# Nine products without a reader between the stages of the first chunk's first joins

## The chip, the cores and the metric

The kernel runs on one core of one Trainium2 chip. The metric is the device time of one execution in microseconds. Beside it stands the profile of one execution, whose span runs from the first recorded instruction to the last.

## The reference

```python
# attention: q, k, v of (4, 8, 768, 48), beta of (4, 8, 768)
k_n = k / (norm(k) + 1e-6)
for t in range(768):                       # one 48 x 48 state for each of 32 heads
    y[t]  = q[t] @ state
    v_old = state^T k_n[t]
    state = state + beta[t] * outer(k_n[t], v[t] - v_old)
# then two matrix products on x = y as (3072, 384)
h = x @ w_in                               # (384, 2048)
out = (h * sigmoid(h)) @ w_out             # (2048, 384)
```

Everything is float32.

## The kernel before

**Tiling.** The 768 tokens of a head are cut into six chunks of 128 tokens, and a chunk into two halves of 64. Inside a half the recurrence is a triangular system, which the kernel solves by inverting triangular blocks. The inverses of blocks of 16 by 16 are made by row updates on VectorE (`invert_first`, L726 to L765, for the first chunk), and are then joined on TensorE: first to blocks of 32, then to blocks of 64. The heads stand in two groups g of 16 heads (two batches each).

**The joins of the first chunk.** `joins(hf)` (L1818) does that for half `hf`, as ten stages in a fixed order:

| Stages | Function | TensorE products, tile | Who takes them out of PSUM |
|---|---|---|---|
| 1, 2 | `corner(0)`, `corner(1)`, L776 | 32 each, 32x32 by 16 columns, L782 | VectorE, two operations each, L789 |
| 3, 4 | `turned(0)`, `turned(1)`, L794 | 16 each, 32x32 by 32, L798 | one on ScalarE, one on VectorE (`by_act`, `by_dve`, L600, L603) |
| 5 | `straight(0)`, L806 | 32, 32x32 by 32, L811 | two on ScalarE, two on VectorE |
| 6 | `merge_half(0, first)`, L858 | 16, 32x32 by 32, L871, `py` | one on each |
| 7 | `straight(1)` | 32 | two on each |
| 8 | `merge_half(1, first)` | 16, `py` | one on each |
| 9, 10 | `merge_half(0, second)`, `merge_half(1, second)` | 16 each, `px` | one on each |

`turned(g)` reads what the evacuation of `corner(g)` wrote; `merge_half(g, first)` reads what that of `turned(g)` wrote; `merge_half(g, second)` reads what the evacuations of `straight(g)` and of `merge_half(g, first)` wrote. After stage 10 `inner` (L900, products `pz`, L905) reads the joined blocks, group 0 and then group 1, and `first_outputs` (L940, `py`, L951) and the transposes of the next chunk (`pt`, L556) follow.

**Float32 products.** A float32 product of TensorE stands in the trace as two MATMUL rows and two LDWEIGHTS rows: the eight products of `busy` in this kernel are x16 rows. Below, a row count is a count of these.

**Order.** The order of every engine's instructions is written out: `pin` (L80) chains each instruction behind the one pinned before it on the same engine. Between the stages of the joins stand other jobs, one entry of a list for each stage. `fetched` puts the loads of the second chunk's queries and of four pieces of `w_in` on the SP queue. `sized` scales a half of `v` on GpSimd (L511, which waits for the last VectorE instruction before it), copies keys there (L613), and begins the next weight piece. A weight piece is brought into shape (`narrow`, L257) by two ScalarE operations (L261, L262; this is what "begin" issues), two VectorE operations (L266, then L270) and one on GpSimd (L274); `fill` takes the oldest piece one step on: `filled(2)` issues L266 here, `filled(1)` issues L270, `begin_next` issues L261 and L262 of a later piece.

**PSUM.** `bank(room, name)` (L63) takes the next bank of a ring. The rings A and CC have three banks each; a join stage takes one of A (evacuated by ScalarE, except in `corner`) and one of CC (evacuated by VectorE). A bank is written again only when its last reader is done.

**`busy(n)`** (L377, matmul at L381) issues n products of the identity with the first state tile, 128x128 by 384 columns, into the next bank of CC. Nothing reads them. Before the change eight of them stand ahead of the joins: three at the start, and five one by one before `corner(0)`.

**Afterwards** the same joins run for the second half (`rest = joins(1)`), cut in pieces by a script (L1925) that puts runs of the first big matrix product (`hidden`, `phid`, L1114, 128x128 by 256, six rows in a run) between them.

Of the kernel before, what the change touches and what calls it, by code (L numbers as in the profile page):

```python
# [19 lines left out]
def kernel(  # L20
# [42 lines left out]
    def bank(room, name):  # L63

        tag = room[0]
        room.rotate(-1)
        return pools.get(tag, banks).tile([P, 512], FP32, name=name, tag=tag)
# [3 lines left out]
    def behind(later, earlier, how=NoSync):  # L71

        tc.add_manual_dep(
            later.ins, earlier.ins.name,
            mybir.DependencyInfo(how, mybir.DependencyReason.DATA), reason="order",
        )
# [3 lines left out]
    def pin(op):  # L80

        engine = op.ins.engine
        if engine in pins:
            behind(op, pins[engine])
        pins[engine] = op
        return op
# [23 lines left out]
    def together(*parts):  # L110
        for _ in zip_longest(*parts):
            pass
# [93 lines left out]
    def deep(fetch, *args, n=2):  # L206

        depth.append(n)
        fetch(*args)
        depth.pop()  # L210
# [166 lines left out]
    def busy(n=1, after=None, how=NoSync):  # L377

        for _ in range(n):
            pw = bank(CC, "pw")  # L380
            done = pin(nc.tensor.matmul(  # L381
                pw[:, 0:DM], lhsT=ident[:],
                rhs=states[0][:].rearrange("p u a d -> p (u a d)"), start=True, stop=True,
            ))
            if after is not None:
                behind(done, after, how)
                after = None
# [470 lines left out]
    def merge_half(g, hf, second):  # L858

        y = ys[0][:, g]  # L860
        pms = [bank(room, "px" if second else "py") for room in (A, CC)]
        for i in range(HH // 2):
            for e in range(2):
                n, k = 2 * i + e, hf ^ e ^ g
                even, odd = slice(W * k, W * k + T), slice(W * k + T, W * (k + 1))
                if second:
                    to, left, right = even, y[odd, n, :], xis[g][odd, n, T:W]
                else:
                    left = aps[0, g][0][even, n // H, n % H, T:W]
                    to, right = odd, xes[0][even, g * HH + n, :]  # L870
                yield pin(nc.tensor.matmul(  # L871
                    pms[k][to, T * i : T * (i + 1)], lhsT=left, rhs=right, start=True, stop=True
                ))
        for k, by in enumerate((by_act, by_dve)):
            e, half = hf ^ k ^ g, slice(W * k, W * k + T) if second else slice(W * k + T, W * (k + 1))
            of = pms[k][half, 0 : HH // 2 * T].rearrange("p (h t) -> p h t", t=T)
            by(xis[g][half, e::2, T:W] if second else y[half, e::2, :], of)
# [808 lines left out]
    def fill(n):  # L1686

        for _ in range(n):
            if not queue:
                return  # L1690
            piece = queue[0]
            piece.begin()
            piece.done += 1
            if piece.done > 1:
                next(piece.steps)
            if piece.done == 3:
                narrowed.append(piece.name)
                queue.popleft()
                for i in freed:
                    fetch_w_out(i)  # L1700
                freed[:] = {
                    ("in", 4): [0], ("in", 5): [1], ("in", 7): [4], ("out", 2): [5], ("out", 3): [6], ("out", 4): [7]
                }.get(piece.name, [])
                if eager and queue and queue[0].name in raws:
                    soon.append(queue[0])
            elif eager and piece.done == 1 and len(queue) > 1 and queue[1].name in raws:
                soon.append(queue[1])
# [110 lines left out]
    def joins(hf, between=()):  # L1818

        for stage in (  # L1820
            corner(0, hf), corner(1, hf), turned(0, hf), turned(1, hf), straight(0, hf), merge_half(0, hf, False),
            straight(1, hf), merge_half(1, hf, False), merge_half(0, hf, True), merge_half(1, hf, True),
        ):
            yield from stage
            for what in between[:1]:
                for one in what if isinstance(what, tuple) else (what,):
                    one()
            between = between[1:]
# [4 lines left out]
    def filled(n):  # L1833
        return lambda: fill(n)

    def fetched():
        deep(load_q, 1, n=3)
        for i in (3, 4, 5, 6):
            deep(fetch_w_in, i)
# [6 lines left out]
    def none():  # L1846
        pass

    together(joins(0, [none, fetched, none, sized, filled(2), none, filled(1), none, begin_next, none]))

    pieces = chained(hidden(0, 0), hidden(0, 1), project())

# [289 lines left out]
```

## Time and profile before

| What | Value |
|---|---|
| Time, median of 3 runs | 620.34 us (620.26 to 621.63) |
| The profiled execution | 622.65 us |
| Its span | 620.9 us |
| Mean granted TensorE clock of the profiled execution | 0.986 |
| TensorE rows MATMUL, LDWEIGHTS | 9538, 9538 |
| Span of the ten stages on TensorE, first start to last end | 26.83 to 41.04 us |

The profiled execution is 1.75 us longer than its span and 2.31 us longer than the median of the runs without a profile. In the rows below, PE is TensorE's matmul, PEld its weight load, DVE VectorE, ACT ScalarE, POOL GpSimd and SP the engine that issues most DMAs. A row of the timeline gives the start, the stretch that the merged instructions cover, engine, line, operation, tile names, shape and count; in brackets stands the idle time before it and what ended it, where "issue" means that the profile shows nothing that the engine waited for. PEclk is the granted TensorE clock as a share of full speed.

### The profile page before, as it was taken

The page shows a single profiled execution, that of the slowest core. Times are in us where ns is not written, and L with a number is a line of the kernel's source. Part 1 is how long each engine was busy: PE and PEld are TensorE (multiplying, and loading weights), DVE is VectorE, ACT ScalarE, POOL GpSimd, SP SyncE. Part 2 cuts the span into 40 slices and gives each one's busy share as a digit, 9 for nine tenths or more (in the row PEclk, how much of TensorE's full clock was granted, in tenths as well). Part 3 has the DMA queues.
Part 4 walks back from the last instruction along what each step waited for, and adds up shares of the span by engine and source line. Part 5 has one row for each costly group of instructions (what it writes and reads, how often), then busy time and mean ns, then how long its engine had stood idle before and what let it go on. Part 6 is the DMA issues. An engine that isn't in the chain of part 4 may idle for free.

```text
span 620.9 us, 21925 instructions
## 1 busy us (share of the span) xinstructions
PE 603.6 (97%) x9538; PEld 528.4 (85%) x9538; DVE 494.8 (80%) x1031; ACT 245.5 (40%) x559; POOL 82.8 (13%) x83
## 2 busy tenths in 40 slices
PE   8779999999999999999999999999999999999997
PEld 5677788766689988998899998898998899998997
DVE  5845888998979986768986859886859898797875
ACT  3654756143361133444332543333534323534500
POOL 5442621246100010000010000010000020000000
PEclk9958999999999999999999999999999999999999
DMA  7845665064426474236064436073533060110002
GB/s 157 183 93 157 207 137 138 29 176 113 108 50 126 87 151 72 61 61 149 0 123 105 111 78 128 1 143 74 124 82 71 1 111 21 35 28 1 1 1 52
DMA packets 144416, 55.07 MB, mean 89 GB/s; under 512 B 113584, under 2 KB 137776, under 8 KB 144320
## 3 DMA queue, kind: packets, MB, share of 16 engines
q1 hardware_dynamic: 143520, 52.80, 38.3%
q8 instruction: 75, 1.23, 0.9%
q10 hardware_dynamic: 800, 0.87, 0.5%
q14 instruction: 21, 0.17, 0.1%
HBM read 40.99 MB, written 10.49 MB: 83 GB/s over the span
## 4 chain that ended last, share of the span: by engine, by line
PE 96%; issue 2%; DVE 1%; ACT 0%; POOL 0%; DVEq 0%; POOLq 0%
PE phid L1114 14%; PE px L1455 14%; PE py L1455 10%; PE hu L1168 10%; PE hx L1168 8%; PE po L1375 7%; PE px L1614 4%; PE pa L585 4%; PE hu L1335 3%; PE hx L1335 3%; PE pz L905 3%; PE ph L893 2%; PE pyc L986 2%; PE pyc L973 2%; PE pu L925 2%
## 5 line engine op out<-in xcount | busy, mean ns | idle before, releaser
L1114 PE MATMUL phid<-xT,w_in 128*128 128x256 f32 x384 | 90.7, 389 | 0.1
L1114 PEld LDWEIGHTS phid<-xT,w_in 128*128 128x128 f32 x384 | 71.7, 192 | 10.9 <-issue 0.7
L688 DVE SCALAR_TENSOR_TENSOR rank<-g,step,x 128x31 f32<-128x31 f32 (+15 forms) x124 | 49.7, 400 | 4.2 <-DMA g<-blocks 1.2
L1455 PE MATMUL px<-sums_of_w,sums_of_g 128*128 128x192 f32 x256 | 46.5, 332 | 0.0
L693 DVE TENSOR_TENSOR x<-x,rank 128x31 f32<-128x31 f32 (+15 forms) x124 | 42.5, 342 | 4.4
L1455 PE MATMUL py<-w_out,sums_of_g 128*128 128x192 f32 x256 | 45.4, 329 | 0.0
L1455 PEld LDWEIGHTS px<-sums_of_w,sums_of_g 128*128 128x128 f32 x256 | 41.4, 190 | 1.2 <-issue 0.7
L1455 PEld LDWEIGHTS py<-w_out,sums_of_g 128*128 128x128 f32 x256 | 41.7, 190 | 0.6 <-issue 0.2
L521 POOL TENSOR_TENSOR vf<-vf,n_slot 128x768 f32<-128x768 f32 x10 | 15.4, 1552 | 190.6 <-DVE sums_of_g L1432 97.2
L1168 PE MATMUL hx<-xT,w_in 128*128 128x256 f32 x144 | 36.0, 379 | 0.0
L600 ACT COPY gT<-hu 128x512 f32<-128x512 f32 x36 | 21.1, 585 | 32.9 <-PE hu L1168 22.9
L1168 PE MATMUL hu<-xT,w_in 128*128 128x256 f32 x144 | 34.0, 379 | 0.0
L600 ACT COPY xT<-pyc 48x128 f32<-48x128 f32 (+2 forms) x120 | 31.1, 259 | 1.6
L932 DVE TENSOR_TENSOR state<-state,pu 48x384 f32<-48x384 f32 x44 | 24.3, 552 | 8.3 <-PE pu L925 7.3
L1168 PEld LDWEIGHTS hu<-xT,w_in 128*128 128x128 f32 x144 | 27.4, 190 | 3.7
L1168 PEld LDWEIGHTS hx<-xT,w_in 128*128 128x128 f32 x144 | 27.3, 190 | 3.6
L1122 ACT ACTIVATE gT<-phid 128x512 f32<-128x512 f32 x24 | 14.4, 600 | 36.6 <-PE phid L1114 34.3
L905 PEld LDWEIGHTS pz<-vf,xi 64*64 64x64 f32 x768 | 25.3, 142 | 3.5 <-issue 3.1
L1183 DVE TENSOR_TENSOR gT<-gT,hx 128x512 f32<-128x512 f32 x24 | 16.4, 685 | 13.3 <-PE hx L1168 13.1
L905 PE MATMUL pz<-vf,xi 64*64 64x48 f32 x768 | 27.0, 226 | 0.0
L1466 DVE TENSOR_TENSOR o<-o,kept 128x192 f32<-128x192 f32 (+1 forms) x24 | 10.1, 422 | 20.1 <-ACT kept L1463 20.0
L1432 DVE TENSOR_TENSOR sums_of_g<-gT 128x512 f32<-128x512 f32 (+2 forms) x36 | 22.6, 662 | 2.3 <-PE py L1455 2.2
(338 smaller groups left out, 1334.9 us busy)
## 6 DMA issues: line engine op xcount, KB each, us to landing
vf<-in_v_dram SPq DMA_DIRECT2D x48, 96.0 KB, 2.7
out_dram<-o SPq DMA_DIRECT2D x36, 96.0 KB, 2.3
w_out<-in_moe_w_in_dram SPq DMA_DIRECT2D x12, 256.0 KB, 3.4
sums_of_w<-in_moe_w_out_dram SPq DMA_DIRECT2D x8, 384.0 KB, 4.2
blocks<-ap SPq DMA_DIRECT2D x40, 64.0 KB, 2.4
g<-blocks SPq DMA_DIRECT2D x4, 512.0 KB
up<-x SPq DMA_DIRECT2D x4, 512.0 KB, 3.2
xi<-up SPq DMA_DIRECT2D x16, 128.0 KB, 3.5
```

Source lines behind the costliest of these rows:

```text
L585: pin(nc.tensor.matmul(pa[e][half, p * n * W : (p + 1) * n * W], lhsT=kq[rows, p, 0, half], rhs=kq[rows, p, js[0] : js[-1] + 1, half], sta ...
L600: return pin(nc.scalar.copy(to, of))
L688: pin(nc.vector.scalar_tensor_tensor(out=tv, in0=g[:, 0:m, m : m + 1].to_broadcast([P, m, n]), scalar=step[:, m : m + 1], in1=x[:, m : m + ...
L693: yield pin(nc.vector.tensor_tensor(out=x[:, 0:m, m:T], in0=x[:, 0:m, m:T], in1=tv, op=ALU.add))
L905: yield pin(nc.tensor.matmul(pz[rows, n * D : (n + 1) * D], lhsT=xis[g][rows, u * H + 2 * p + e, :], rhs=vfs[c][rows, hf, g * HB + u, p, : ...
L932: pin(nc.vector.tensor_tensor(out=to, in0=to, in1=by_heads(pu[of]), op=ALU.add))
L1114: pin(nc.tensor.matmul(ph[:, j * GT : (j + 1) * GT], lhsT=w_in[:, a, (2 * f + j) * P : (2 * f + j + 1) * P], rhs=xTs[c, hf][:, a, :], star ...
L1168: pin(nc.tensor.matmul(to[:, GT * i : GT * (i + 1)], lhsT=weights[:, f], rhs=moving, start=start and i == 0, stop=True, skip_group_check=True,
L1335: pin(nc.tensor.matmul(to[:, GT * i : GT * (i + 1)], lhsT=weights[:, 2 * u + i], rhs=moving, start=start and i == 0, stop=True, skip_group ...
L1375: pin(nc.tensor.matmul(pos[i][:, 0:DM], lhsT=hidden_of(0, hf, f // 2)[:, at : at + C], rhs=w_outs[f // HFF][:, f % HFF, :], start=(f == 0) ...
L1455: pin(nc.tensor.matmul(to, lhsT=at, rhs=quarter(f, *b) if isinstance(b, tuple) else sums_of_w[b][:, f], start=start and n == 0, stop=n == ...
L1614: pin(nc.tensor.matmul(acc, lhsT=hidden_at(g)[:, r], rhs=out_weights_at(w)[:, r], start=start and r == 0, stop=r == 3, skip_group_check=Tr ...
```

## The change

A tuple of two jobs takes the place of one in three entries of the list: after stage 2, `fetched` is followed by `busy(4)`; after stage 4, `sized` is followed by `busy(3)`; after stage 7, `filled(1)` is followed by `busy(2)`. The list is that of the first half; the joins of the second half are as before. No other instruction is added or taken away. Each of the nine products takes the next bank of the ring CC, so the banks of CC that the later stages get are others than before.

```diff
+    def steadied(n):
+        return lambda: busy(n)
+
...
-    together(joins(0, [none, fetched, none, sized, filled(2), none, filled(1), none, begin_next, none]))
+    together(joins(0, [none, (fetched, steadied(4)), none, (sized, steadied(3)), filled(2), none, (filled(1), steadied(2)), none, begin_next, none]))
```

`joins` ran a tuple's entries one after the other before the change already.

## The prediction

> **What bounds the kernel now.** I read the page first, for its engine table, its slices, its queues and its chain.
>
> ```profile
> PE 603.6 (97%) x9538; PEld 528.4 (85%) x9538; DVE 494.8 (80%) x1031; ACT 245.5 (40%) x559; POOL 82.8 (13%) x83
> ...
> PEclk9958999999999999999999999999999999999999
> ...
> q8 instruction: 75, 1.23, 0.9%
> ...
> PE 96%; issue 2%; DVE 1%; ACT 0%; POOL 0%; DVEq 0%; POOLq 0%
> ```
>
> TensorE bounds the kernel: 96% of the chain that ended last is PE, so time lost or won on PE early on is still there at the end. The granted clock is low only in slices 3 and 4 (15.5 us each); the joins of the first half lie there. Next comes the timeline of PE through those joins and `inner`.
>
> ```profile
> 27.79 1.03 PE L782 MATMUL pl<-sums_of_w,ap 32*32 32x16 f32 x94 [0.48 <-issue]
> 28.75 1.44 PE L798 MATMUL pl<-sums_of_w 32*32 32x32 f32 x33
> 32.12 0.95 PE L798 MATMUL pl<-sums_of_w 32*32 32x32 f32 x26 [1.93 <-issue]
> ...
> 36.40 1.00 PE L811 MATMUL pl<-sums_of_w 32*32 32x32 f32 x57 [1.58 <-issue]
> ...
> 39.90 1.14 PE L871 MATMUL px<-xi,xe_y 32*32 32x32 f32 x32 [0.98 <-DVE xe_y L603]
> 40.97 3.54 PE L905 MATMUL pz<-vf,xi 64*64 64x48 f32 x62
> ```
>
> PE stands still for 1.93, 1.58 and 0.98 us, the first two times for nothing that the profile names. The table of the stretches between these stops shows what they share.
>
> ```profile
> 27.79:30.20 2.41, 2.37 (x127) 2.20 (x127) 1.88 (x6) 0.81 (x2) 2.41 (x3) 1.00 0.57 118
> 32.12:34.82 2.70, 2.70 (x128) 2.56 (x128) 1.00 (x3) 1.54 (x3) 2.34 (x3) 0.50 0.55 103
> 36.40:38.92 2.52, 2.52 (x127) 2.39 (x126) 1.84 (x5) 1.16 (x4) 0.83 (x1) 0.50 0.63 127
> ```
>
> (Columns: stretch, length, busy time and count of PE, PEld, DVE, ACT, POOL, then PEclk, DMA share, GB/s.) Each holds 127 or 128 matmuls. On the page, the queue q8 carries instructions in 75 packets; 9538 + 9538 PE rows over 75 are 254, or 127 matmuls with their loads. I read the stops as PE without instructions: a block of 127 matmuls is used up in 2.4 to 2.7 us, but blocks begin 32.12 - 27.79 = 4.33 and 36.40 - 32.12 = 4.28 us apart. The third stop ends with VectorE's `xe_y`.
>
> The clock is the second thing. Single microseconds date its turns:
>
> ```profile
> 30.00:31.00 1.00, 0.19 (x5) 0.14 (x3) 0.42 (x1) 0.36 (x1) 1.00 (x2) 0.92 0.76 143
> 44.00:45.00 1.00, 1.00 (x51) 1.00 (x53) 0.34 (x2) 0.00 (x0) 0.00 (x0) 0.75 0.40 79
> 54.00:55.00 1.00, 0.78 (x28) 0.77 (x28) 0.38 (x1) 0.33 (x2) 0.00 (x0) 0.87 0.65 193
> 58.00:59.00 1.00, 1.00 (x8) 0.95 (x7) 0.00 (x0) 0.71 (x2) 0.00 (x0) 0.93 0.26 90
> ```
>
> With 0.50 as the low value, 0.92 puts the drop at 30.84 and 0.75 the rise at 44.50; 0.87 and 0.93 give a second dip from 54.74 to 58.14. The first lasts 13.66 us, the second 3.40, a quarter of it.
>
> **The change part by part.** *Added on PE:* nine products, 18 rows of 128x128 by 384. Their length comes from the big product's runs and from the rows of `pw` itself.
>
> ```profile
> 55.27 2.93 PE L1114 MATMUL phid<-xT,w_in 128*128 128x256 f32 x6
> ...
> 60.36 1.56 PE L1114 MATMUL phid<-xT,w_in 128*128 128x256 f32 x6
> ```
>
> ```profile
> L381 PE MATMUL pw<-state,ident x16: 486/590/1009, 2.1 to 26.4; 128*128 128x384 f32 x16
> ```
> The run of six in the second dip takes 2.93 - 1.56 = 1.37 us more than one at full clock: 0.23 us a row of 256 columns, and 0.34 for 384. The upper end is 0.49, the shortest `pw` row by itself. I take 0.34, since rows of a series overlap, and 0.1 for each series' start: 2.8, 2.1 and 1.5 us, together 6.4. At half clock a row costs 0.68, and 18 of them 12.2.
>
> *What lies beside them.* I carry the stages forward with the row spacings of before: `turned` 0.028 us ((0.95 - 0.24) / 26), `straight` 0.0135, the merges 0.017 at full clock (below: 1.13 for 56 rows) and 0.029 at half. Instruction blocks still begin at 32.12 and 36.40, but each boundary lies earlier among the stages, by 8, 14 and 18 rows.
>
> ```profile
> 68.00 1.13 PE L871 MATMUL px<-xi,xe_y 32*32 32x32 f32 x56
> ```
>
> - *Four products* take the place of `turned(0)` at 28.75 and end at 31.55. VectorE's evacuation of `corner` is done by then, so the third product's bank is free. 24 rows of `turned(0)` run to 32.2, and the next block is there at 32.12: the stop of 1.93 us is filled. `turned(1)` ends at 33.3 (33.0 before).
> - *Three products* run to 35.4. They need the banks that VectorE empties of `turned`, 0.42 us of work on an idle engine. `straight(0)` ends at 36.3, 2.4 us later than before. 18 of the 32 rows of the first merge are in the old block; they end at 36.6, after 36.40, so the stop of 1.58 us is gone too. `straight(1)` ends at 37.7, 0.5 us late.
> - *Two products* start at 37.8. Here VectorE is late next, and its queue is:
>
> ```profile
> 34.23 0.87 DVE L603 COPY xi<-pl 32x256 f32<-32x256 f32 x2 [0.62 <-PE pl L811]
> 35.12 1.34 DVE L266 TENSOR_SCALAR w_in<-w_in 128x768 uint32<-128x768 uint32 x1
> 36.50 0.43 DVE L603 COPY xe_y<-py 32x256 f32<-32x256 f32 x1
> 37.53 0.86 DVE L603 COPY xi<-pl 32x256 f32<-32x256 f32 x2 [0.60 <-PE pl L811]
> 38.43 0.96 DVE L270 SCALAR_TENSOR_TENSOR w_in<-sums_of_w_in,w_in 128x768 uint32<-128x768 uint32 x1
> 39.42 0.43 DVE L603 COPY xe_y<-py 32x256 f32<-32x256 f32 x1
> ```
>
> It begins at 36.55, 2.3 us later, and has no pause: 36.55 + 0.87 + 1.34 + 0.43 + 0.86 + 0.96 + 0.43 = 41.45, where before it ended at 39.85. This is 1.6 us later, because two pauses of 0.6 are used up. The second product waits for the bank of the first merge (39.2), the merge behind it for the bank that VectorE empties of `straight(1)` (40.05); both lie beside this queue. `merge_half(1, second)` starts at 41.5 in place of 39.90.
>
> *The clock.* Why it falls is read from three stretches of the length of the short dip, each ending at a turn:
>
> ```profile
> 27.43:30.84 3.41, 2.37 (x127) 2.20 (x127) 2.63 (x6) 1.49 (x3) 3.41 (x4) 1.00 0.56 112
> 51.32:54.74 3.42, 2.59 (x115) 2.26 (x115) 1.52 (x5) 0.65 (x2) 0.00 (x0) 1.00 0.45 132
> 41.08:44.49 3.41, 3.41 (x72) 3.41 (x75) 0.91 (x2) 0.83 (x2) 0.29 (x1) 0.50 0.65 120
> ```
>
> Ahead of both drops PE was busy for 70 to 76%, with 32x32 tiles nearly alone; ahead of the rise it was full, with 64x64. In the new order the stretches from 27.43, 30.84, 34.26 and 37.67 hold 2.1, 1.6, 1.1 and 1.3 us of full-array rows, so I take the clock as held. Then `merge_half(1, second)` takes 0.55 in place of 1.07 and ends at 42.05. The rows of `pz` take 0.027 in place of (3.54 - 0.30) / 61 = 0.053 us.
>
> *Behind the joins.* ScalarE brings the next wait:
>
> ```profile
> 39.22 0.88 ACT L261 ACTIVATE w_in<-w_out 128x768 f32<-128x768 f32 x1
> 40.01 0.97 ACT L262 ACTIVATE w_out<-w_out,plus 128x768 int32<-128x768 uint32 x1
> 41.08 0.36 ACT L600 COPY xi<-px 32x256 f32<-32x256 f32 x1
> ```
>
> L261 and L262 stand between its evacuations of the two second merges and last 1.76 us. Before, the stop of 0.98 us covered them. Now the first of these evacuations runs from 41.3 to 41.65, the pair to 43.35, the second to 43.75. Group 0 of `pz` runs from 42.05 to 42.9; group 1 waits until 43.8 and ends at 44.8 with its drain, against 44.51 before. **Sum: 0.3 us later.** With 0.49 a row the same walk ends 1.3 us later; with L266 at half its length (POOL idle) and no wait on ScalarE, 0.6 earlier.
>
> On GpSimd the scaling of `v` (L511) moves with the VectorE instruction ahead of it by under 1 us; `pz` needs it only after 42. The SP queue keeps its order, the products issue no DMA, and no load waits for them. Behind `pz`, PE is full (chain above), so 0.3 us stays. The sum is made on the profiled execution, 622.65 us with a span of 620.9 to become 621.2; the median of the runs is 2.31 us lower, and I add the 0.3 to that: **620.6 us.**
>
> [...] No row here shows the supply itself; the distance of 127 matmuls speaks for it.
>
> **The rivals.**
> 1. *Forecast:* stops filled, clock held through the joins, new waits on VectorE and ScalarE; second dip as before. +0.3 us; -0.6 to +1.3.
> 2. *The second dip goes as well.* The 3.42 us ahead of it hold small tiles nearly alone, between a `phid` run with transposes and the next run. With the stages 0.3 us later, full-array rows of its edge fall into that stretch. +0.3 - 1.37 = -1.1, 619.3 us. For it: the small tiles last barely as long as the 3.4 us between two turns. Against: the move is small.
> 3. *More than that:* the second dip goes and ScalarE and VectorE don't hold `pz` (-0.6 - 1.37 = -2.0), 618.4 us.
> 4. *The clock dips after the joins, slower:* at full clock `pz` fills only half of the stretch 41.08 to 44.49, where at half clock it filled all of it. If that is too little, the clock falls at 44.5 for one window, over the transposes:
>
> ```profile
> 44.50:47.91 3.41, 1.75 (x14) 1.51 (x15) 1.00 0.49 154
> ```
>
> (PE and PEld rows of L556 alone.) 14 rows of 128 columns are 1792, against 1536 that cost 1.37 us in the second dip: 1.6 us more. +1.9, 622.2 us. [...]
> 5. *The clock isn't held:* products at 0.68 a row from 30.84 on. `turned(1)` ends at 33.9, the three products at 38.0, `straight(1)` at 40.6, two products at 43.3, the merges at 45.8; then `pz` is 3.0 (full clock) to 4.7 us late. +3.9, 624.2 us. Against: 1.1 us or more of dense rows in each window.
> 6. *The change doesn't do what it says:* the stops aren't instruction supply and stay where the stages are. 1.6 + 1.93 + 1.58 = 5.1 later at the last merge, less 0.5 and 0.8 by the clock: +3.8, 624.1 us.
>
> **How the numbers follow.** Chances: 0.45, 0.20, 0.08, 0.12, 0.08, 0.07. A measurement of this kernel can tell about 0.3%, 1.9 us, from no change. Faster: case 3 and a seventh of case 2, 0.11. Slower: cases 5 and 6 and somewhat over half of case 4, 0.22. Within: 0.67. The range from 618.5 to 622.9 takes in cases 1, 2, 4 and most of 3, and leaves out 5 and 6.
>
> **What would show it.** Right: no stop marked issue between 31 and 37; PEclk 1.00 from 30 to 44; `pw` rows about 0.34 apart; `merge_half(1, second)` at about 41.5 behind DVE; group 1 of `pz` behind ACT at about 43.8. Wrong: PEclk 0.50 while products run (case 5) or right after 44.5 (case 4); stops of 1.5 us or more at the old stages (case 6); PEclk 1.00 from 54 to 58 (cases 2, 3). The sum is wrong, too, if instruction blocks arrive later than at 32.12 and 36.40.

## The result and the profile after

| Comparison | Changed | Before, same chip | Ratio (95% interval) |
|---|---|---|---|
| First | 627.58 us (median of 4, 626.06 to 628.46) | 620.41 us (4) | 1.0102 (1.0076 to 1.0128) |
| Again, `after_again` | 624.10 us (12, 622.28 to 628.27) | 620.69 us (30, 617.64 to 624.85) | 1.0054 (1.0026 to 1.0082) |

The change makes the kernel slower, by 0.5% where more runs were taken. Forecast was 620.6 us, no difference that can be told. The first ratio is the larger, but it rests on four executions of each kernel: in the second row single executions of the kernel before spread over 7 us, while the first four happened to lie within 1.4. The ratios are not quotients of the two medians, and differ from them by up to 0.2%.

The page of the changed kernel, in the lines that were read first before:

```profile
PE 608.8 (97%) x9556; PEld 530.2 (85%) x9556; DVE 494.3 (79%) x1031; ACT 245.9 (39%) x559; POOL 82.8 (13%) x83
...
PEclk9897999999999999999999999999999999999999
...
q8 instruction: 75, 1.23, 0.8%
...
PE 96%; issue 2%; ACT 1%; DMA 1%; DVE 1%; SPq 0%; DVEq 0%
```

The span is 625.8 us. PE has its 18 rows more. The clock's digit of the third slice (31.3 to 46.9 us) is 9 in place of 5, but those of the second and the fourth are 8 and 7, in place of 9 and 8. "issue" still has 2% of the chain: if the stops in the joins are gone, others have come. The timeline of PE through the joins:

```profile
28.59 2.85 PE L381 MATMUL pw<-state,ident 128*128 128x384 f32 x8
31.36 2.00 PE L798 MATMUL pl<-sums_of_w 32*32 32x32 f32 x64
33.30 2.20 PE L381 MATMUL pw<-state,ident 128*128 128x384 f32 x6
35.43 0.92 PE L811 MATMUL pl<-sums_of_w 32*32 32x32 f32 x52
...
37.69 1.95 PE L381 MATMUL pw<-state,ident 128*128 128x384 f32 x4
...
40.10 1.55 PE L871 MATMUL px<-xi,xe_y 32*32 32x32 f32 x59
41.58 1.28 PE L905 MATMUL pz<-vf,xi 64*64 64x48 f32 x34
43.39 1.07 PE L905 MATMUL pz<-vf,xi 64*64 64x48 f32 x29 [0.54 <-ACT xi L600]
```

No row here is marked issue: the stops of 1.93 and 1.58 us are filled. The products stand where the forecast put them, `pz` starts at 41.58, waits 0.54 us for ScalarE, and ends at 43.39 + 1.07 = 44.46; before it ended at 40.97 + 3.54 = 44.51. **At 44.5 us the two kernels are level.** All that is lost is lost behind the joins. The view of waits of PE from there to the end, first of before:

```profile
PE pu L925 <- issue: 0.9, 1, 0.9
PE px L1455 <- issue: 0.6, 1, 0.6
PE px L847 <- issue: 0.5, 1, 0.5
PE pl L798 <- issue: 0.5, 1, 0.5
PE pyc L973 <- issue: 0.4, 2, 0.2
PE pyc L986 <- issue: 0.4, 1, 0.4
...
PE py L871 <- issue: 0.3, 1, 0.3
```

and of the changed kernel (us in total, times, longest):

```profile
PE pyc L986 <- issue: 1.6, 1, 1.6
PE pyc L973 <- issue: 1.2, 1, 1.2
PE pl L782 <- issue: 1.2, 1, 1.2
PE pz L905 <- issue: 1.0, 1, 1.0
PE pl L798 <- issue: 0.9, 1, 0.9
PE py L871 <- issue: 0.8, 1, 0.8
...
PE px L847 <- issue: 0.3, 1, 0.3
PE py L951 <- issue: 0.2, 1, 0.2
```

The sums are 3.6 us before and 7.2 after. The stops are other ones, at other lines. The rest of the 4.9 us between the two spans is a dip of the clock, 6.83 us long where before it was 3.40:

```profile
56.15:62.98 6.83, 6.83 (x58) 5.72 (x55) 1.38 (x2) 3.24 (x5) 1.84 (x1) 0.50 0.44 134
```

By the 1.37 us that 3.40 us of dip cost before, its second half is worth about 1.4: 3.6 + 1.4 = 5.0. This dip isn't the change's: in `after_again` the clock is low only from 19.2 to 22.6 us, and its stops behind the joins still sum to 6.4. That profiled execution took 622.33 us, less than the one of before (622.65): it is the second shortest of its twelve, without the 3.40 us of dip that before has behind its joins. Two single profiles therefore don't show the loss; the medians do, and the profiles show where PE stops.

**Which stops they are.** Number all of PE's records in the trace in order of their starts, from the program's first: MATMUL, LDWEIGHTS and the 148 semaphore and drain instructions between them. Every stop marked issue behind the joins, in both kernels, lies at a number that leaves 193 or 194 when divided by 256; in the experiments they do too (192 where a record is missing). The 75 packets of q8 are 16.4 KB each (1.23 MB / 75), and 2 x 9538 + 148 = 19224 records of PE before are 256 to a packet. I read the stops so: PE comes to the end of a block of 256 instructions and the next isn't there. The times of the packets in the trace say so as well. Take packets and blocks in order: in 159 of the 160 stops marked issue from 12 us on, in the 18 profiles other than e2_four's, PE goes on 0.9 to 1.8 us (median 1.4) behind the end of the packet with the next block, and no block in these profiles is begun sooner behind its packet. So the stops, those before the change too, are instruction supply. Now the largest one, before row 2255 of the MATMUL rows (counted from 0). Before:

```profile
86.87 0.94 PE L925 MATMUL pu<-z,kb 64*48 64x48 f32 x64
87.63 1.08 PE L986 MATMUL pyc<-ap,z 64*48 64x64 f32 x64
88.63 3.03 PE L1114 MATMUL phid<-xT,w_in 128*128 128x256 f32 x12
```

After:

```profile
90.16 0.94 PE L925 MATMUL pu<-z,kb 64*48 64x48 f32 x64
90.91 0.96 PE L986 MATMUL pyc<-ap,z 64*48 64x64 f32 x55
93.52 0.33 PE L986 MATMUL pyc<-ap,z 64*48 64x64 f32 x9 [1.65 <-issue]
```

The same stage now breaks off after 55 of its 64 rows. With 18 rows more ahead of it, the block ends 9 rows before the end of `pyc`; before, it ended 18 rows later, nine rows into `phid`. Rows of `phid` are (3.03 - 0.39) / 11 = 0.24 us apart (0.39 is one row's mean in the page's `phid` group), so the block ended 0.1 + 9 x 0.24 = 2.3 us later against the same stages. The records of q8 place the packet with the next block at 88.35 to 89.28 before and at 91.25 to 92.18 after. Before, the block was needed at 88.63 + 9 x 0.24 = 90.8, 1.5 us behind its packet: no stop. After, it was needed at 91.9, and PE went on at 93.52, 1.34 us behind the packet. The DMA view of the changed kernel, 86 to 95 us, shows what is on the engines then:

```profile
q1 hardware_dynamic: 2788, 1.10, 50.1%
q8 instruction: 2, 0.03, 1.5%
...
w_out<-in_moe_w_out_dram SPq DMA_DIRECT2D x2, 384.0 KB, 5.5
```

Two loads of 384 KB take 5.5 us each to land, beside two instruction packets. So theory A, formed from these rows: *18 added rows move the ends of all later blocks; some come to lie where the next packet is not yet there, because it stands beside data loads.* Theory B: what is lost is the price of the products' work. Theory C: it is the clock around the joins.

### The profile page after: what moved, and what is told of

The parts are those of the page before. It is cut to its first block, busy times and chain, and to the rows that moved or that the text cites. A ratio compares the mean times of both kernels' runs of the same rounds, so it can differ in the third digit from the quotient of the medians.

```text
span 625.8 us, 21961 instructions
## 1 busy us (share of the span) xinstructions
PE 608.8 (97%) x9556; PEld 530.2 (85%) x9556; DVE 494.3 (79%) x1031; ACT 245.9 (39%) x559; POOL 82.8 (13%) x83
## 3 DMA queue, kind: packets, MB, share of 16 engines
q8 instruction: 75, 1.23, 0.8%
## 4 chain that ended last, share of the span: by engine, by line
PE 96%; issue 2%; ACT 1%; DMA 1%; DVE 1%; SPq 0%; DVEq 0%
PE phid L1114 14%; PE px L1455 14%; PE py L1455 10%; PE hu L1168 10%; PE hx L1168 8%; PE po L1375 7%; PE px L1614 4%; PE pa L585 4%; PE hu L1335 3%; PE hx L1335 3%; PE pz L905 2%; PE ph L893 2%; PE pyc L973 2%; PE pw L381 2%; PE pyc L986 2%
## 5 line engine op out<-in xcount | busy, mean ns | idle before, releaser
L1432 DVE TENSOR_TENSOR sums_of_g<-gT 128x512 f32<-128x512 f32 (+2 forms) x36 | 22.6, 663 | 2.3 <-PE py L1455 2.2
```

## The experiments

Stops behind the joins are the sum of the lines marked issue of PE's view of waits from about the end of `pz` on. "Rows" are the MATMUL rows by which a kernel moves the block ends behind 60 us. Each kernel ran on one chip beside the kernel before.

| Kernel | Rows | Median us (runs) | Before us | Ratio (95% interval) | Stops behind the joins, us |
|---|---|---|---|---|---|
| before | 0 | | | | 3.6 |
| changed, first profile | 18 | 627.58 (4) | 620.41 | 1.0102 (1.0076 to 1.0128) | 7.2 |
| e1_tiny | 18 | 625.09 (10) | 621.61 | 1.0059 (1.0032 to 1.0086) | 5.1 |
| e2_four | 8 | 623.10 (10) | 621.61 | 1.0022 (0.9998 to 1.0047) | no view |
| e6_light_before | 0 | 622.68 (10) | 621.61 | 1.0016 (0.9998 to 1.0034) | 3.9 |
| e7_light_after | 18 | 625.90 (7) | 621.61 | 1.0053 (1.0025 to 1.0081) | 4.1 |
| after_again | 18 | 624.10 (12) | 620.69 | 1.0054 (1.0026 to 1.0082) | 6.4 |
| e8_pad | 128 | 626.81 (7) | 620.69 | 1.0102 (1.0067 to 1.0137) | 2.6 |
| e5_short | 1 | 621.93 (12) | 620.69 | 1.0033 (1.0008 to 1.0058) | 3.8 |
| e3_no_early | 2 | 623.92 (12) | 620.69 | 1.0043 (1.0013 to 1.0073) | 5.5 |
| e9_start18 | 18 | 626.06 (12) | 620.79 | 1.0067 (1.0037 to 1.0096) | 5.8 |
| e10_exact | 0 | 621.66 (12) | 620.79 | 1.0006 (0.9978 to 1.0034) | 3.6 |
| e11_short_early | -8 | 620.03 (12) | 620.79 | 0.9975 (0.9948 to 1.0003) | 2.2 |
| e12_late18 | 18 | 624.05 (12) | 620.83 | 1.0044 (1.0014 to 1.0074) | 5.1 |
| e13_behind18 | 18 | 623.52 (12) | 620.83 | 1.0042 (1.0016 to 1.0068) | 5.5 |
| e14_short_early | -8 | 619.60 (12) | 620.83 | 0.9972 (0.9949 to 0.9995) | 1.6 |
| e15_late2 | 2 | 623.09 (12) | 621.02 | 1.0031 (1.0003 to 1.0058) | 3.9 |
| e16_late10 | 10 | 623.30 (12) | 621.02 | 1.0019 (1.0000 to 1.0039) | 3.7 |
| e17_short_late | 0 | 620.80 (12) | 621.02 | 1.0013 (0.9992 to 1.0034) | 4.1 |

One execution of e2_four took 1223.54 us and one of e15_late2 1542.76; nothing here explains them, the ratios leave them out, and the first is the one whose profile was taken, so it has no stops to compare.

**e1_tiny: the same rows with almost no work.** The nine products have 4 columns in place of 384.

```diff
-                pw[:, 0:DM], lhsT=ident[:],
+                pw[:, 0:cols], lhsT=ident[:],
...
+        return lambda: busy(n, cols=4)
```

> The nine products stand at the same places and in the same banks, but are 4 columns wide in place of 384: the same 18 rows and the same instruction blocks, almost no work. Theory A (the 18 rows move the block ends behind the joins, so that instructions are fetched behind the weights' loads): slower than before by 3 to 7 us, with stops of 1 us or more at rows 193 to 194 of a block between 49 and 94 us. Theory B (the 6 us of work of the products and their waits are the price): within 1 us of before. Theory C (the dense rows move the clock's windows): within 1 us of before, with the first dip as in before.

Measured: 1.0059, as much as the change. The price of the work isn't what is lost: B falls as the main cause. The clock was low from 18.4 to 25.2 and from 32.0 to 49.1 us here, and held through the joins in the changed kernel; both are slower by as much, which speaks against C.

**e2_four: the first series alone.** Eight rows.

```diff
-none, (sized, steadied(3)), filled(2), none, (filled(1), steadied(2)), none,
+none, sized, filled(2), none, filled(1), none,
```

> Only the four products after the second stage; 8 rows in place of 18. Theory A: block ends 8 rows earlier than before, so the stops behind the joins are others again; anything from 0 to 6 us slower, with the whole loss in stops and dips behind 44 us. Theory B: 2.8 of 6.4 us of work, so about 3 us slower than before, lost ahead of 44 us. Theory C: clock falls during the joins as in before, within 1 us.

Measured: 1.0022, an interval that just takes in 1. Between no change and the change, and no more can be said.

**e6_light_before, e7_light_after: fewer bytes near 50 us.** Pieces 3 to 5 of `w_in` load only 32 of 256 columns, without the change and with it; the rest of those pieces is cleared to zero, so part of the product is left out.

```diff
+        n = 2 * WF if i < 3 or i > 5 else 64
-            in_line(nc.sync.dma_start(out=raw[:, a], in_=src[:, a]))
+            in_line(nc.sync.dma_start(out=raw[:, a, 0:n], in_=src[:, a, 0:n]))
```

> Before, with the loads of three pieces of w_in (numbers 3 to 5, between 44 and 60 us) cut to 32 of 256 columns, so that their weights are wrong; the rooms are cleared by GpSimd at the start. A reference for the run that does the same with the change. Theory A: the fetches between 44 and 60 us come within 1 us of a block's start, so faster than before by 0 to 2 us. Theories B and C: within 1 us of before.

> The change, with the same three pieces cut to 32 of 256 columns (their weights are wrong). Theory A: no stop at the block end near 50 us, the block of 45 us is fetched within 1.5 us; at most 3 us slower than the reference run with light loads (what stays are collisions behind 60 us). Theory B: 6 to 7 us slower than that run, as the change is slower than before. Theory C: the second dip as long as in the change, 2 to 4 us slower than that run.

Measured: 622.68 and 625.90. The stop at L782 near 50 us, 1.2 us in the first profile of the changed kernel, is absent in e7. That shows nothing of the loads: with all columns loaded it is absent in `after_again` too, and in e1. And the 3.2 us between e7 and e6 stay. The stop near 50 us is not what makes the change slow; e7 still has 1.9 us at `pyc` and 0.9 at the other `pyc` line.

**e8_pad: all block ends back where they were, one block on.** The change with 110 rows of tiny products near 60 us, 128 in all.

```diff
-                busy(n)
+                pw = bank(CC, "pw")
+                for _ in range(n):
+                    pin(nc.tensor.matmul(
+                        pw[0:T, 0:4], lhsT=ident[0:T, 0:T], rhs=ident[0:T, 0:4], start=True, stop=True,
+                    ))
...
-        "... b r q r f j4 j4 ..."
+        "... b r q r x55 f j4 j4 ..."
```

> The change, and behind the third run of the first big product (near 60 us) 55 tiny products (32x32 by 4 columns, 110 rows), so that the added rows are 18 + 110 = 128, one whole instruction block: from there on all block ends fall where they fell before. Their own price is 110 rows of about 0.014 us, 1.5 us. Theory A: the stop near 90 us is gone or under 0.4 us, and the stops between 240 and 430 us are those of before; so no slower than the change, 0.5 to 2 us faster. Theory B (work of the products) and C (clock): 1.5 us slower than the change.

Measured: 1.0102, a miss as a repair. The stops fell to 2.6 us, and those before rows 2255 and 4413 are gone, as A says. But the tiny products stand on PE from 58.84 to 62.79 us, 3.95 us where 1.5 were expected: their rows lie 0.032 us apart and not 0.014. The clock was low for 6.8 us as well (61.7 to 68.5). The repair costs more than the loss, so the time of this run decides nothing between the theories.

**e5_short, e3_no_early: nearly no rows more.** In e5 all 17 products are made of two-byte elements, which gives one row each (x8 for eight such products in e14's trace, 0.48 us a row): one row more in all. In e3 the eight early ones are left out: two rows more.

```diff
-                pw[:, 0:DM], lhsT=ident[:],
-                rhs=states[0][:].rearrange("p u a d -> p (u a d)"), start=True, stop=True,
+                pw[:, 0:512], lhsT=ident[:].bitcast(BF16)[:, 0:P],
+                rhs=states[0][:].rearrange("p u a d -> p (u a d)").bitcast(BF16)[:, 0:512], start=True, stop=True,
```

```diff
-        for _ in range(n):
+        for _ in range(n if joining else 0):
```

> All seventeen unread products as single rows of 512 columns of two bytes: 17 rows in place of 34, so 1 more than before behind the joins, with block ends one row from those of before; a series lasts 0.2 us a product in place of 0.65. Theory A: within 1.5 us of before, no stop over 0.5 us near 90 us. Theory B: 1.9 us of work in place of 6.4, so 1 to 2 us slower than before. Theory C: the clock falls in the joins as before if the short series are too little; within 1.5 us of before.

> The nine products, without the eight that stood ahead of the joins: 2 rows more than before behind the joins, the same number of products but one. Theory A: within 2 us of before once the start is taken out (start to joins may change by 0 to 2 us, since PE idles there and the clock may be low); no stop over 0.5 us near 90 us. Theory B: as slow as the change, 4 to 7 us over before. Theory C: slower than the change by what a low clock at the start costs.

Measured: 1.0033 and 1.0043. The stop before row 2255 is gone in e5, as A says; in e3 0.48 us of it is left, in `phid`, and the one before row 4413 is gone in both. But both are slower than before. In e3's profile the joins also take longer, 16.46 us from the first `pl` to `pz` (14.1 before), with the clock low from 29.7 to 33.1 us. Either one or two rows already move some end to a bad place, or the products do cost; e15 takes this up.

**e9_start18: 18 rows at the very start.** Ten tiny products stand for the first of the early ones.

```diff
-    busy(3)
+    for _ in range(10):
+        pin(nc.tensor.matmul(
+            pw[0:T, 0:4], lhsT=ident[0:T, 0:T], rhs=ident[0:T, 0:4], start=True, stop=True,
+        ))
+    busy(2)
```

> Before, with nothing added in the joins. At the very start, where PE waits for the keys, one of the three unread products is replaced by ten tiny ones (32x32 by 4 columns): 18 rows more, as in the change, in idle time. Theory A (block ends): behind 70 us the stops of the change come back (1.5 to 2.1 us before row 2255, 1.1 to 1.8 before row 4413), and the stretch from the first state update (about 70 us) to the end is 1 to 3 us longer than before; in all 1.5 to 3.5 us slower than before. Theories B and C (work of the products, clock in the joins): within 0.7 us of before.

Measured: 1.0067. The stops of the change are back (5.8 us behind the joins) without anything in the joins; but the clock was low from 12.7 to 29.8 us as well, so it isn't clean.

**e10_exact: dense products, no ends moved.** The early eight are short as in e5, and four products of 512 columns stand in the joins.

```diff
+                pin(nc.tensor.matmul(
+                    pw[:], lhsT=ident[:], rhs=ident[:].unsqueeze(1).to_broadcast([P, 4, P]), start=True, stop=True,
+                ))
...
+(fetched, steadied(2)) ... (sized, steadied(1)) ... (filled(1), steadied(1))
```

> Dense products in the joins without a moved block end: two, one and one products of 512 float32 columns (8 rows) in place of four, three and two, and the eight early ones as single rows of 512 columns of two bytes (8 rows fewer): net 0 rows behind the joins. Theory A: no stop over 0.5 us near row 2237, and from 70 us on as before; with the clock held in the joins 0 to 2 us faster than before, 3 to 5 us faster than the change. Theory B: 3.4 us of work in place of 6.4, so 1 to 3 us slower than before. Theory C: the clock's dip behind the joins decides, within 2 us of before.

Measured: 1.0006. Four dense products that move no end cost nothing that can be told. That isn't clean either: against e11, next, which has the short early products alone, e10 is 0.3% slower, by its four products and by eight rows.

**e11_short_early, e14_short_early: the early eight short, nothing else.** The diff of e5 in the kernel before, without products in the joins; the same kernel, on two chips.

> Before, with the eight early products as single rows of 512 columns of two bytes and nothing in the joins: 8 rows fewer. The reference for the run above. All theories: the start up to the joins 0 to 1 us shorter or the same. Theory A: block ends 8 rows later behind the joins, so other stops, within 2 us of before. Theories B and C: within 1 us of before.

> The kernel with short early products and nothing in the joins, once more. All theories allow it; if block ends 8 rows later suit this kernel, 1 to 2 us faster than before again, else within 0.7 us of before.

Measured: 0.9975 and 0.9972, the second with an interval below 1. It is the best version here, faster than both kernels, by about the 0.3% that can be told at all. What is left of its stops in e14:

```profile
PE px L873 <- issue: 0.9, 1, 0.9
PE pyc L975 <- issue: 0.4, 1, 0.4
...
PE pu L927 <- issue: 0.3, 1, 0.3
```

**e12_late18, e13_behind18: the rows alone.** Nine tiny products of 32x32 by 4 columns, 18 rows, in the kernel before: near 60 us in e12 (the edit of e8 with x9, without the change), and between stage 10 and `pz` in e13, whose edit this is:

```diff
-    together(joins(0, [none, fetched, none, sized, filled(2), none, filled(1), none, begin_next, none]))
+    together(joins(0, [none, fetched, none, sized, filled(2), none, filled(1), none, begin_next, tiny]))
```

> Before, with nine tiny products (32x32 by 4 columns, 18 rows, about 0.25 us) behind the third run of the first big product, near 60 us; start and joins as before. Theory A (block ends): the stops before rows 2255 and 4413 are back, and the stretch from the first state update to the end is 1 to 2.5 us longer than before; 1 to 2.5 us slower in all. Theories B and C: 0.25 us slower, and the stops of before.

> Before, with the same nine tiny products behind the tenth stage of the joins, ahead of pz (41 us); start and joins as before. Theory A: all that the change loses behind the joins: 2.5 to 4 us slower than before, with the stops before rows 2255 and 4413. Theories B and C: 0.3 us slower.

Measured: 1.0044 and 1.0042, against the change's 1.0054. What e12 adds is 18 short matmuls, 17 of them in this row:

```profile
58.37 0.69 PE L1956 MATMUL pw<-ident 32*32 32x4 f32 x17
```

and what it gets for it:

```profile
85.41 0.94 PE L925 MATMUL pu<-z,kb 64*48 64x48 f32 x64
86.17 0.96 PE L986 MATMUL pyc<-ap,z 64*48 64x64 f32 x55
88.99 0.33 PE L986 MATMUL pyc<-ap,z 64*48 64x64 f32 x9 [1.85 <-issue]
```

The same stage breaks off after the same 55 rows. The packet came at 86.55 to 87.49. The view of waits of e12, from the end of `pz`, has the lines of the changed kernel from there on:

```profile
PE pyc L986 <- issue: 1.9, 1, 1.9
PE pyc L973 <- issue: 1.2, 1, 1.2
...
PE pz L905 <- issue: 0.7, 1, 0.7
PE py L871 <- issue: 0.7, 1, 0.7
...
PE px L847 <- issue: 0.6, 1, 0.6
```

Since e12 moves nothing ahead of its tiny products, near 60 us, and loses about as much as e13, what is lost lies behind them.

Two rivals for this pair can be judged by other rows. *The tiny products have a price of their own:* e12's rows stand on PE for 0.6 us (0.032 us apart), and in e13 the way from the start of the last `px` stage to `pz` takes 1.79 us in place of 1.07. Without that, 2.6 of e12's 3.2 us and 2.0 of e13's 2.7 are left. *They also take one bank of the ring CC, so that all later banks are others.* But the change and e1 take nine banks, whole turns of the ring of three, and e9 none more, and they are as slow; and e17, below, takes one and isn't slower than the kernel before.

**The two stops in all profiles.** The changed kernel and e12 have a second stop in common, before row 4413. In the kernel before the block that ends there holds 16 large rows, 2.8 us of work; with 18 rows more it holds only short ones, of `pz` and `pyc`. First before, then the changed kernel:

```profile
243.34 2.87 PE L1455 MATMUL px<-w_out,gT 128*128 128x192 f32 x16
```

```profile
248.81 0.21 PE L973 MATMUL pyc<-kq,state 48*48 48x64 f32 x1 [1.25 <-issue]
```

Before row 2255 the seven profiles with 18 rows stop for 1.34 to 1.92 us, before row 4413 for 0.90 to 1.79; the two together make 2.8 to 3.4 us in each. Ten rows (e16) make 0.65 and 0.33. No profile with eight rows fewer, with none or with one has either stop. The records of q8 tell the two apart. At row 4413 the packet isn't late: in the changed kernel it starts 1.2 us after PE has entered the block before (1.2 in the kernel before too), but that block is used up in 2.2 us. At row 2255 it is late: with 18 rows it starts 2.5 to 3.2 us after that, in all other profiles 0.0 to 1.5. With 18 rows the second 384 KB load goes out within 0.3 us of PE's entry into that block; where a load comes ahead of it in the others, it goes out 1.4 to 2.0 us before the entry. That speaks for the loads, but no run changed them. So theory A holds in its first half, the moved ends; its "because it stands beside data loads" is argued at row 2255 and not so at row 4413.

**e15_late2, e16_late10, e17_short_late: how much by how many rows.** The edit of e12 with one and with five tiny products; and e11 with four tiny ones near 60 us, which puts all later ends back where they were before.

```diff
-        "... b r q r x9 f j4 j4 ..."
+        "... b r q r x1 f j4 j4 ..."
```

(x5 in e16, x4 in e17, there with the diff of e5 in the kernel before.)

> The kernel before with one tiny product (32x32x4, two rows) after the third run of phid, near 60 us; nothing in the joins. Theory A (the added rows move the ends of the instruction blocks behind them; 18 rows cost 0.4%): two rows move them by two rows only, so at most a ninth of that if the cost grows evenly, a ratio from 0.999 to 1.002, and no stop of over 1 us near 88 to 94 us. If single rows can already put a fetch behind another load, 1.003 to 1.0045, as in the two kernels with one and two net rows in the joins (1.0033 and 1.0043). Theory B (what those two kernels lost is their work in the joins): 0.999 to 1.001 here.

> The same with five tiny products, ten rows. Theory A with a cost that grows evenly: 1.002 to 1.003. Theory A with collisions that come and go by the place of a block's end: anything from 0.997 to 1.006, told by which stops stand in the trace. If moved ends cost nothing: 1.000.

> The kernel with the eight early products short (eight rows fewer; 0.9975 and 0.9972) and four tiny products near 60 us, eight rows, so that every block ends from there on where it ends before the change. If that kernel's gain comes from the eight rows by which later ends move: about 1.000. If it comes from the shorter work ahead of the joins or from the ends up to 60 us: 0.997 to 0.998.

Measured: 1.0031, 1.0019 and 1.0013. In e16 the break moves just as counted:

```profile
89.30 1.08 PE L986 MATMUL pyc<-ap,z 64*48 64x64 f32 x63
91.02 0.21 PE L986 MATMUL pyc<-ap,z 64*48 64x64 f32 x1 [0.65 <-issue]
```

18 - 10 = 8 rows later than with 18, 63 rows in place of 55, and the stop is 0.65 us in place of 1.34 to 1.92. With two rows more (e15) or none, `pyc` isn't broken. e17's stops are those of before again (4.1 against 3.6 us), and most of e11's gain goes with them. And e15, with two rows and nothing in the joins, is slower by about as much as e5 and e3: the work in the joins isn't needed for that, though its interval nearly touches 1 and which end these two rows bring into trouble isn't seen. The time doesn't grow evenly with the rows; it goes by where single ends fall.

## Why the prediction was wrong

- **The price of the products held.** Rows of a series lie 0.32 us apart in the changed kernel's timeline (0.34 forecast); the series last 2.77, 2.13 and 1.90 us (2.8, 2.1 and 1.5 forecast; in the third the second product starts 0.61 us after the row ahead of it).
- **The stops in the joins were instruction supply, and are filled.** No stop marked issue lies between 31 and 37 us; the last rival falls. The distance between such stops, multiples of 256 of PE's instructions, confirms the reading of 127 matmuls a packet, and the stops at 32.12 and 36.40 ended 1.25 and 1.47 us behind the end of a packet of q8.
- **The clock was held through the joins**, in the changed kernel (low only from 18.6 to 22.0 and from 56.2 to 63.0 us in the first profile), in `after_again` and in e7; rivals 4 and 5 fall. All eleven profiles without dense products in the joins have it low there for a time; of the six with float32 ones only e3, without the early eight, does.
- **The new waits came where they were put**, a little earlier, since L266 took 0.69 us and not 1.34:

```profile
37.51 0.69 DVE L266 TENSOR_SCALAR w_in<-w_in 128x768 uint32<-128x768 uint32 x1
...
39.48 0.96 DVE L270 SCALAR_TENSOR_TENSOR w_in<-sums_of_w_in,w_in 128x768 uint32<-128x768 uint32 x1
40.47 0.43 DVE L603 COPY xe_y<-py 32x256 f32<-32x256 f32 x1
```

```profile
41.32 0.90 ACT L261 ACTIVATE w_in<-w_out 128x768 f32<-128x768 f32 x1
42.13 0.96 ACT L262 ACTIVATE w_out<-w_out,plus 128x768 int32<-128x768 uint32 x1
42.99 0.34 ACT L600 COPY xi<-px 32x256 f32<-32x256 f32 x1
```

VectorE ends at 40.90 (41.45 forecast), ScalarE's second evacuation starts at 42.99 (43.35), group 1 of `pz` at 43.39 (43.8). `pz` ends at 44.46 where 44.8 was forecast. One reason given for VectorE's delay is misread: of the two pauses of 0.6 us one lies ahead of the queue that is summed, and the 2.3 us become 1.6 by the other and four gaps under 0.05. The sum itself holds.
- **The second dip** (rivals 2 and 3) was twice as long in the first profile (6.83 us, 3.40 before) and absent in `after_again`: it comes and goes by the execution.
- **The step that failed is "Behind `pz`, PE is full, so 0.3 us stays".** The text had counted that each block boundary lies 8, 14 and 18 rows earlier among the stages, and used it only inside the joins. It holds for every boundary behind them, some 65 more. PE was read as full from the chain's 96%; but a full PE stays full only while its next block is there, and before the change that was so by small margins (0.2 us at row 2255, if PE goes on 1.3 us behind its packet). Nothing was put down for these boundaries. What the runs showed there: two new stops of 2.8 to 3.4 us together; e12 and e13, by their times without their own price, put the moved ends at 2.0 to 2.6 us, and e16 shows one of them row by row. What is left of the change's 3.4 us (624.10 - 620.69) can't be told from the forecast's 0.3.
- **The rivals lacked this case.** All of them but the last ended at the clock or at `pz`, and the closing sentence on late blocks had only those at 32.12 and 36.40 in mind.

Most ends of a block cost little here: in the kernel before 13 of 74 crossings stop PE by over 0.15 us, in the changed one 9. But the stops behind the joins sum to 1.6 to 7.2 us by the table above, and 18 rows decide which they are and how long they last.

**What stays open.** The stops of the seven profiles with 18 rows average 5.6 us, those of before, e6, e10 and e17 3.8: a difference of 1.8, of the 2.7 to 3.4 that the medians of the change, e12 and e13 show. Behind `pz` little else is lost: take from the time between the end of `pz` and the end of the span all waits of PE over 0.15 us, 0.4 us for each us of low clock there (1.37 / 3.40) and the tiny products that stand there, and 569.5 to 571.6 us are left in all 18 profiles, where the times themselves run from 574.6 to 581.2. How long the start and the joins take differs between executions, so the rest of the medians' differences can't be placed. That the packet near 91 us is late because of the loads beside it is argued from the DMA view and the times of issue; loads at that place were not changed. What one or two rows do (e5, e3, e15), how much of the first ratio was chance, and the two long executions are not settled.

## What to carry to other kernels

When instructions are added to an engine that bounds the kernel, count by how many the ends of its instruction blocks (256 instructions here) move against all later stages, not only at the place of the edit; a block that used to end in large products may now end in a run of small ones, which are used up far faster (0.24 us a row of `phid` here, 0.014 a row of `pyc`). Test it with the same number of instructions and no work, at another place: if that costs as much, the edit's own idea isn't what failed. And where fillers are wanted, try the fewest rows that do it: here eight rows fewer, with shorter work in them, were the only edit that came out faster, by 0.3%, with an interval below 1 in one of its two groups.

## What the runs showed of the hardware

- The stops of PE marked issue behind the joins lay at the same place of every 256 of its instructions, 193 or 194, with 256 to a packet of q8. The longest stop lasted 2.2 us (e16, at `pa`); in 159 of the 160 from 12 us on PE went on 0.9 to 1.8 us behind the end of the packet.
- A block of small products can be used up before the next is there without any packet being late: 2.2 us for the block ahead of row 4413, whose next packet started 1.2 us into it, took 0.9 and was in use 1.3 us later.
- The packet ahead of row 2255 started 2.5 to 3.2 us into the block before where a 384 KB load went out within 0.3 us of that block's start, and 0.0 to 1.5 us into it elsewhere.
- The granted clock fell to 0.50 for stretches of 13.65 and 3.41 us in the profile of before, and the place of such stretches differs between executions of one kernel: in `after_again` only 19.2 to 22.6, in the first profile of the same kernel 18.6 to 22.0 and 56.2 to 63.0 (3.41 and 6.83 us).
- With the clock the time of one kernel spreads: the kernel before ran from 617.62 to 627.07 us over 145 runs, beside the five groups above; the 23 runs with a mean clock of 0.989 have a median of 618.94, the 27 with 0.983 621.79, and the 9 with 0.980 or less 625.39. Four runs within 1.4 us said little of that.
